# The lead of a top-k attention and mixture-of-experts kernel: the order of the first key and weight pieces

## The chip, the cores and the metric

The kernel runs on one core of a Trainium2 chip. The metric is the device time of one execution in microseconds, as a median over repeated runs. One further execution was taken by the hardware profiler, and all rows below are from that one.

## The reference

Three layers follow one another: attention that keeps only the 32 largest scores of each row, a dense layer that takes the larger of three products, and a layer of eight experts of which each token uses one.

```python
# q, k, v: (4, 8, 576, 64); out: (2304, 512)
scores = scale * np.matmul(q, k.transpose(0, 1, 3, 2))
kth = np.partition(scores, -top_k, axis=-1)[..., -top_k:-top_k + 1]      # top_k = 32
scores = np.where(scores >= kth, scores, -1e9)
attn = np.exp(scores - np.max(scores, axis=-1, keepdims=True))
attn = attn / (np.sum(attn, axis=-1, keepdims=True) + 1e-09)
x = np.matmul(attn, v)                          # heads side by side: (2304, 512)
h = np.maximum(np.maximum(x @ w1, x @ w2), x @ w3)                        # 512 -> 768
x = h @ w_out                                                             # 768 -> 512
logits = x @ w_gate                                                       # 8 experts
expert_idx = np.argmax(logits, axis=1)
# each token: gate_w * (max(x @ w1[e], 0) @ w2[e]) for its one expert e (512 -> 1024 -> 512)
```

The dense weights arrive as 64-bit floats, since they were scaled by a 64-bit number. All else is 32-bit.

## The kernel before

The attention is cut into 144 tiles. A full tile is 128 query rows of one head of one batch entry; the last 64 rows of two heads make up a pair tile. Batch entry 0 comes first, and its first eight tiles are query block 0 of heads 0 to 7, so tile n is head n there. The main loop runs over a clock t, and each pass issues one step of each of many stages, each stage on another tile: the scores of tile t+2 (`st_scores`, L883), the copy of the scores of tile t+1 from PSUM to SBUF by ScalarE (`st_evac`, L896), the eight largest of six chunks of tile t on VectorE (`st_chunks`, L904), the rounds that go on from these, the mask, the exponential, the product with the values, and units of the two dense layers and of the experts. The order is written by hand. Each engine takes its own instructions strictly in the order in which they are issued, and waits in place where an input is missing; the same holds for the queue on SyncE that issues nearly all DMAs.

`after(n, f)` (L671) puts a step off to n clocks later, `bulk` and `tail_bulk` collect VectorE's instructions of one clock, and `run_bulk` (L695) issues them: those in `bulk` first, those in `tail_bulk` behind.

Keys, queries and weights are used as pairs of 16-bit numbers, a high part and a low part. A key or query piece takes four steps: a load into a staging tile (`stage_load`, `stage_load2`), the high part by ScalarE (L757), the low part by VectorE (L734 in the lead, L741 with one more ScalarE copy at L740 later on), and one clock later a DMA transpose that SyncE issues (L772, L779 and L793). The query gets a swapped copy by two more DMAs (L797), which ScalarE issues in the lead. `prep_k(b, i)` (L760) has five pieces for each batch entry: pieces 0 and 1 hold the first 512 keys of heads 0 to 3, pieces 2 and 3 those of heads 4 to 7, piece 4 the last 64 keys of all heads. They are called k0 to k4 below, and the first query piece is called q0.

A dense weight piece (`prep_w`, L835) is 512 columns of 64-bit numbers, 512 KB. There are 24 of them, called w0 to w23 below, and six buffers for their raw bits. VectorE rebuilds a 32-bit number by three integer instructions into PSUM (L859, L862, L864, the "bits"), one clock later ScalarE writes the high part (L868), and the low part is made in one of two ways: in the lead by VectorE (L870), later by a ScalarE copy into the raw buffer (L874) and a subtraction on GpSimd (L875). From t = 0 to 5 two weight pieces are loaded in each pass, later one; each is worked on one pass after it was loaded.

The lead (L1552 to L1576) is what runs at negative clocks ahead of the main loop. It starts the loads of q0, k4, k0, k1, k2 and k3 at once, then does one piece in each clock, then w0 and w1, and at clock -1 it issues the scores and the copy of tile 0. The high and low parts of the lead's pieces lie in work buffers (`split_tile`, L747): three of the kind "e" and two of the kind "f", so the sixth piece has to take the buffer of the fourth.

## Time and profile of the kernel before

| | |
|---|---|
| median of 3 runs | 956.38 us (955.54 to 957.42) |
| the profiled execution | 951.46 us, of which its span from first to last instruction is 949.7 us |
| mean granted TensorE clock | 0.960 of full speed |
| VectorE / TensorE / ScalarE / GpSimd busy | 80% / 79% / 73% / 64% of the span |

The page divides the span into engines' busy times. An average over stages says little here, since the first three quarters and the last quarter are worked by different engines; the stretches and the orders of time below show which. Times of rows are microseconds from the span's start, the end of a row's bracket names what ended the engine's idle time before the instruction. PE is TensorE, DVE is VectorE, ACT is ScalarE, POOL is GpSimd, SP is SyncE; a q behind the name marks what the engine's queue issues, DMAs above all.

### The profile page before, as it was taken

The page shows a single profiled execution, that of the slowest core. Times are in us where ns is not written, and L with a number is a line of the kernel's source. Part 1 is how long each engine was busy: PE and PEld are TensorE (multiplying, and loading weights), DVE is VectorE, ACT ScalarE, POOL GpSimd, SP SyncE. Part 2 cuts the span into 40 slices and gives each one's busy share as a digit, 9 for nine tenths or more (in the row PEclk, how much of TensorE's full clock was granted, in tenths as well). Part 3 has the DMA queues.
Part 4 walks back from the last instruction along what each step waited for, and adds up shares of the span by engine and source line. Part 5 has one row for each costly group of instructions (what it writes and reads, how often), then busy time and mean ns, then how long its engine had stood idle before and what let it go on. Part 6 is the DMA issues. An engine that isn't in the chain of part 4 may idle for free. (4 is left out here: it accounts for less than half of the span.)

```text
span 949.7 us, 29065 instructions
## 1 busy us (share of the span) xinstructions
PE 751.6 (79%) x10606; PEld 578.1 (61%) x10606; DVE 762.5 (80%) x3110; ACT 694.3 (73%) x1463; POOL 608.6 (64%) x552
## 2 busy tenths in 40 slices
PE   0212368888777899878898998889999999999992
PEld 0100237666555677657677787567887767588881
DVE  4999999999998999998998899788972335567671
ACT  2668899997898988898897997887863231466661
POOL 1457798998988789787877898687985221111110
PEclk9999999999998999899989999889999999999996
DMA  9681977775996788699969888687799358699270
GB/s 229 204 260 29 223 158 153 138 143 105 184 165 151 143 161 175 111 206 176 173 128 179 170 139 154 131 188 127 170 168 156 91 150 278 177 299 279 63 216 16
DMA packets 372164, 155.93 MB, mean 164 GB/s; under 512 B 331931, under 2 KB 348319, under 8 KB 372000
## 3 DMA queue, kind: packets, MB, share of 16 engines
q1 hardware_dynamic: 368128, 143.10, 71.9%
q0 software_dynamic: 3136, 9.46, 2.8%
q8 instruction: 87, 1.43, 0.6%
q10 hardware_dynamic: 736, 1.32, 0.5%
q14 instruction: 77, 0.63, 0.3%
HBM read 76.06 MB, written 16.67 MB: 98 GB/s over the span
## 5 line engine op out<-in xcount | busy, mean ns | idle before, releaser
L355 PEld LDWEIGHTS <-W 128*128 128x128 f16 x4560 | 248.2, 100 | 28.0 <-issue 25.2
L965 POOL TENSOR_TENSOR f<-s,g 128x576 f32<-128x576 f32 x144 | 200.9, 1395 | 69.6 <-DVE vec L974 32.9
L355 PE MATMUL mm<-xT,W 128*128 128x128 f16 x3456 | 210.5, 222 | 18.2 <-DVE W1h L741 6.8
L1058 POOL TENSOR_TENSOR phl<-e,phl 128x576 f16<-128x576 f32 x144 | 186.3, 1293 | 8.1 <-ACT phl L1054 7.9
L913 DVE MAX8 c<-s 128x8 f32<-128x96 f32 x864 | 175.2, 243 | 8.3 <-ACT s L899 4.7
L892 PEld LDWEIGHTS <-qT 128*128 128x128 f16 (+1 forms) x640 | 56.3, 108 | 188.9 <-issue 156.6
L892 PE MATMUL S<-kt,qT 128*128 128x64 f16 (+3 forms) x320 | 62.4, 345 | 109.9 <-ACT s L899 94.4
L1077 PE MATMUL av<-vh,pt 128*128 128x65 f16 (+3 forms) x1600 | 112.4, 201 | 17.4 <-DVE xn L1126 12.9
L1043 ACT ACTIVATE e<-s,be 128x576 f32<-128x576 f32 x144 | 110.6, 768 | 7.7 <-POOL phl L1058 5.7
L974 DVE MAX8 vec<-f 128x8 f32<-128x576 f32 x144 | 108.8, 755 | 5.3 <-POOL f L965 1.4
L959 ACT ACTIVATE g<-s,bf 128x576 uint16<-128x576 f32 x144 | 111.1, 771 | 0.1
L1048 DVE SCALAR_TENSOR_TENSOR e<-s,hkth,e 128x576 f32<-128x576 f32 x72 | 104.1, 1446 | 8.3 <-ACT e L1043 8.1
L1077 PEld LDWEIGHTS <-pt 128*128 128x128 f16 (+3 forms) x2400 | 90.8, 104 | 30.5 <-issue 17.6
L1054 ACT ACTIVATE phl<-e 128x576 f16<-128x576 f32 x144 | 97.4, 676 | 11.3 <-DMA pt<-phl 11.3
L899 ACT ACTIVATE s<-S 128x576 f32<-128x576 f32 x144 | 92.3, 641 | 15.5 <-PE S L892 14.6
L1077 PE MATMUL av<-vl,pt 128*128 128x64 f16 (+3 forms) x800 | 101.6, 199 | 0.0
L1037 POOL TENSOR_TENSOR s<-s,g 128x576 f32<-128x576 f32 x72 | 95.9, 1331 | 0.3
L456 DVE SCALAR_TENSOR_TENSOR W<-st,W 128x1024 f16<-128x1024 f32 x56 | 65.8, 1220 | 36.7 <-ACT W L455 34.6
L892 PE MATMUL S<-kT,qT 128*128 128x512 f16 (+3 forms) x320 | 48.5, 293 | 18.7 <-ACT s L899 18.7
L455 ACT ACTIVATE W<-st 128x1024 f16<-128x1024 f32 x56 | 55.6, 1046 | 1.8 <-DMA st<-in_moe_w_dram 1.8
L1034 ACT ACTIVATE g<-s,hkth 128x576 uint16<-128x576 f32 x72 | 55.4, 769 | 0.0
L1161 POOL TENSOR_TENSOR hhl<-a,hhl 128x384 f16<-128x384 f32 x36 | 34.7, 964 | 28.9 <-ACT hhl L1160 28.9
(232 smaller groups left out, 1586.4 us busy)
## 6 DMA issues: line engine op xcount, KB each, us to landing
st<-in_moe_w_dram SPq DMA_DIRECT2D x72, 512.0 KB
st<-in_moe_w_dram SPq DMA_DIRECT2D x28, 256.0 KB
raw<-in_moe_w_dram SPq DMA_DIRECT2D x12, 512.0 KB
st<-in_v_dram SPq DMA_DIRECT2D x16, 256.0 KB
hs<-he SPq DMA_DIRECT2D x16, 256.0 KB
hTe<-hs SPq DMA_DIRECT2D x8, 512.0 KB
st<-in_q_dram SPq DMA_DIRECT2D x15, 256.0 KB
qT<-qT SPq DMA_DIRECT2D x30, 128.0 KB
```

The costliest lines, as they stand in the source:

```text
L355: nc.tensor.matmul(out=ps[:, o * n:(o + 1) * n], lhsT=w(b, kk, c), rhs=x(a, kk), start=(kk == 0 and i == 0), stop=(kk == KD - 1 and i == 2))
L892: nc.tensor.matmul(out=ps[o:o + m, j, 0:(REM if j else NQ * P)], lhsT=qt[:, vv, hh, 0:m], rhs=kr[:, hh] if j else km[:, hh // HG, :, hh % HG],
L913: nc.vector.max(out=c[:, i * 8:(i + 1) * 8], in_=s[:, i * CW:(i + 1) * CW])
L959: nc.scalar.activation(out=gg[n], in_=Ss[n], func=ACTF.Sign, bias=bf[g][:, i], accum_out=cnt[g][:, i])
L965: nc.gpsimd.tensor_tensor(out=ff[n], in0=Ss[n], in1=gg.pop(n).bitcast(F16), op=ALU.subtract)
L974: bulk.append(lambda: nc.vector.max(out=y8[g][:, i, 1:9], in_=y))
L1037: nc.gpsimd.tensor_tensor(out=Ss[n], in0=Ss[n], in1=zz.pop(n).bitcast(F16), op=ALU.subtract)
L1043: nc.scalar.activation(out=e, in_=Ss.pop(n) if early(n) else Ss[n], func=ACTF.Exp, scale=ESC, bias=be[g][:, i])
L1048: nc.vector.scalar_tensor_tensor(out=e, in0=Ss.pop(n), scalar=kth[g][:, i:i + 1], in1=e, op0=ALU.is_ge, op1=ALU.mult)
L1054: nc.scalar.activation(out=ph[:, 0, 0:S], in_=p, func=ACTF.Copy)
L1058: nc.gpsimd.tensor_tensor(out=ph[:, 1, 0:S], in0=p, in1=ph[:, 0, 0:S], op=ALU.subtract)
L1077: nc.tensor.matmul(out=av[o:o + m, i, 0:n], lhsT=t[0:kk, p * NCH + c, o:o + m], rhs=v_rows(x, b, c, hh)[:, 0:n], start=(c == 0 and p == 0 ...
```

## The change

The lead starts the loads of q0, k4, k0 and k1, then of w0, then of k2. It works through these six in the order q0, k4, k0, k1, w0, k2, one in each clock from -8 on. At clock -4 it starts the loads of w1 and of k3, and leaves their remaining steps to the main loop: both are worked on in the pass t = 0, and k3 is transposed in the pass t = 1. The branch by which VectorE made the low parts of the lead's weight pieces is gone, so w0 and w1 take the way of the others: a ScalarE copy and a subtraction on GpSimd.

```diff
--- before.py
+++ after.py
@@ -61,7 +61,7 @@
     NSWAP, XLAG, KLAG, TSTOP, EARLY_RATE, LATE_RATE = 4, 2, 2, 140, 1.4, 1.8
     RANK_LAG = 1
     ZN, NFB, NGB = (2,), 2, 4
-    NWL, WARM, ST = 2, 4, 3
+    WARM, ST = 4, 3
     ESC = 1.0 / (float(D) ** 0.5 * SC * SC * DOWN)
     LSC = 1.0 / (SC * SC)
     X2SC = 1.0 / (SC * SC)
@@ -855,7 +855,6 @@
                     lw, hw = raw[:, :, 0], raw[:, :, 1]
                     f = ps_m.tile([P, 512], F32, tag="mm", name="bits")
                     bits = f.bitcast(I32)
-                    head = clock[0] < 0
                     bulk.append(lambda: nc.vector.tensor_scalar(
                         out=bits, in0=hw, scalar1=3, scalar2=0x3FFFFFF8,
                         op0=ALU.logical_shift_left, op1=ALU.bitwise_and))
@@ -866,10 +865,6 @@
 
                     def rest():
                         nc.scalar.activation(out=dst[:, 0], in_=f, func=ACTF.Copy, scale=SC)
-                        if head:
-                            nc.vector.scalar_tensor_tensor(out=dst[:, 1], in0=f, scalar=SC, in1=dst[:, 0],
-                                                           op0=ALU.mult, op1=ALU.subtract)
-                            return
                         whole = raw.rearrange("p f w -> p (f w)")[:, 0:512].bitcast(F32)
                         nc.scalar.activation(out=whole, in_=f, func=ACTF.Copy, scale=SC)
                         nc.gpsimd.tensor_tensor(out=dst[:, 1], in0=whole, in1=dst[:, 0], op=ALU.subtract)
@@ -1533,6 +1528,10 @@
             preps.sort(key=lambda it: it[0])
             wq = [(prep_w, (i,)) for i in range(NPW + KF)]
 
+            def begin_w():
+                f, a = wq.pop(0)
+                return f(*a)
+
             def ok(n):
                 return 0 <= n < NTL
 
@@ -1549,13 +1548,20 @@
                 for ph in phl:
                     nc.gpsimd.memset(ph[:, :, S:SPAD], 0.0)
 
+                def begin(it):
+                    return it[2](*it[3])
+
                 lead = [it for it in preps if it[0] < 0]
                 lead.sort(key=lambda it: (it[2] is prep_k, (it[3][1] + 1) % (NQ + 1) if it[2] is prep_k else 0))
-                clock[0] = -len(lead) - 4
-                pend, pend_p, pend_w, lead_w, wq_n = [], [], [], [], [0]
                 for it in lead:
                     preps.remove(it)
-                    pend.append(it[2](*it[3]))
+                rows = lead[0], lead[1], lead[2], lead[3]
+                rest_k = lead[4:]
+                clock[0] = -8
+                pend_p, pend_w = [], []
+                pend = [begin(it) for it in rows]
+                pend.append(begin_w())
+                pend.append(begin(rest_k[0]))
                 while clock[0] < 0:
                     if clock[0] == -1:
                         st_scores(0)
@@ -1564,16 +1570,13 @@
                         f()
                     if pend:
                         pend.pop(0)()
-                    elif lead_w:
-                        lead_w.pop(0)()
-                    if len(pend) < NWL and wq_n[0] < NWL:
-                        wq_n[0] += 1
-                        f, a = wq.pop(0)
-                        lead_w.append(f(*a))
+                    if clock[0] == -4:
+                        pend_w.append(begin_w())
+                        pend_p.append(begin(rest_k[1]))
                     run_bulk()
                     run_late()
                     clock[0] += 1
-                assert not (pend or lead_w or any(c < 0 for c in due))
+                assert not (pend or any(c < 0 for c in due))
                 st_scores(1)
                 t = -1
                 second = None
```

## Rows read from the trace of the kernel before

**Rows 1.** The page's part 1: busy time, share of the span, instructions of each engine.

```profile
PE 751.6 (79%) x10606; PEld 578.1 (61%) x10606; DVE 762.5 (80%) x3110; ACT 694.3 (73%) x1463; POOL 608.6 (64%) x552
```

**Rows 2.** Busy time by stretch: start:end, length, each engine's busy us (instructions), clock, DMA.

```profile
23.60:100.00 76.40, 17.67 (x75) 7.67 (x75) 73.87 (x264) 55.02 (x122) 44.20 (x38) 1.00 0.59 172
...
700.00:800.00 100.00, 99.61 (x1250) 73.38 (x1247) 36.95 (x142) 33.46 (x66) 35.79 (x43) 1.00 0.65 154
```

**Rows 3.** VectorE's waits from 23.6 to 700: us in total, times, longest.

```profile
DVE bits L859 <- DMA raw<-in_moe_w_out_dram: 0.9, 1, 0.9
```

**Rows 4.** Order of time, ScalarE, 7 to 25: start, us, line, names, idle before.

```profile
7.15 0.63 ACT L757 ACTIVATE f<-s 128x512 f16<-128x512 f32 x1 [0.21 <-DMA s<-in_k_dram]
8.00 0.63 ACT L757 ACTIVATE f<-s 128x512 f16<-128x512 f32 x1 [0.22 <-DMA s<-in_k_dram]
9.64 1.18 ACTq L797 DMA_DIRECT2D qT<-qT  x2
15.26 0.63 ACT L757 ACTIVATE f<-s 128x512 f16<-128x512 f32 x1 [6.63 <-DMA kt<-f]
18.95 0.60 ACT L868 ACTIVATE W<-bits 128x512 f16<-128x512 f32 x1 [3.06 <-DVE bits L864]
22.37 0.60 ACT L868 ACTIVATE W<-bits 128x512 f16<-128x512 f32 x1 [2.82 <-DVE bits L864]
22.86 0.64 ACT L899 ACTIVATE s<-S 128x576 f32<-128x576 f32 x1
24.72 0.65 ACT L899 ACTIVATE s<-S 128x576 f32<-128x576 f32 x1 [1.21 <-PE S L892]
```

**Rows 5.** Order of time, SyncE's DMA issues, 5 to 13 (the same columns).

```profile
5.43 1.59 SPq L793 DMA_TRANSPOSE qT<-e  x1
...
9.77 1.44 SPq L779 DMA_TRANSPOSE kt<-f  x1
11.26 1.03 SPq L844 DMA_DIRECT2D raw<-in_moe_w_dram  x1
```

**Rows 6.** Order of time, VectorE, 23 to 43 (the same columns).

```profile
23.61 1.05 DVE L913 MAX8 c<-s 128x8 f32<-128x96 f32 x6
25.40 0.42 DVE L913 MAX8 c<-s 128x8 f32<-128x96 f32 x2 [0.74 <-ACT s L899]
...
26.77 0.68 DVE L859 TENSOR_SCALAR bits<-raw 128x512 int32<-128x512 int32 x1
...
28.86 0.69 DVE L859 TENSOR_SCALAR bits<-raw 128x512 int32<-128x512 int32 x1
...
30.91 0.41 DVE L913 MAX8 c<-s 128x8 f32<-128x96 f32 x2
...
39.87 0.69 DVE L859 TENSOR_SCALAR bits<-raw 128x512 int32<-128x512 int32 x1
...
41.92 0.68 DVE L741 TENSOR_TENSOR hl<-mm,hl 128x512 f16<-128x512 f32 x1
```

**Rows 7.** Busy time by stretch, 8 to 30 (last two columns: DMA share, GB/s).

```profile
8.00:15.00 7.00, 0.00 (x0) 0.00 (x0) 1.19 (x2) 0.63 (x1) 0.00 (x0) 1.00 1.05 195
15.00:20.00 5.00, 1.12 (x4) 0.56 (x5) 3.20 (x5) 1.23 (x2) 0.00 (x0) 1.00 1.14 269
20.00:25.00 5.00, 1.12 (x4) 0.46 (x4) 3.92 (x11) 1.42 (x3) 0.00 (x0) 1.00 0.93 329
25.00:30.00 5.00, 2.24 (x8) 0.91 (x8) 4.57 (x18) 2.04 (x4) 0.00 (x0) 1.00 1.10 346
```

**Rows 8.** Order of time, GpSimd and VectorE, 26 to 39.

```profile
26.22 0.19 DVE L929 MATCH_REPLACE8 c<-T,c 128x48 f32<-128x48 f32 x1
...
36.64 2.27 POOL L875 TENSOR_TENSOR W<-raw,W 128x512 f16<-128x512 f32 x2 [1.77 <-DMA raw<-in_moe_w_dram]
...
37.24 0.19 DVE L929 MATCH_REPLACE8 c<-T,c 128x48 f32<-128x48 f32 x1
```

**Rows 9.** Order of time, TensorE: the scores of tile 4.

```profile
32.81 1.12 PE L892 MATMUL S<-kt,qT 128*128 128x512 f16 x4 [4.42 <-ACT s L899]
```

## The prediction

> **What bounds the kernel now.** First the page's table of engines: VectorE is busy for 80% of the span and TensorE for 79% [rows 1], which as an average names no bound. The table by stretch does: from 23.6 to 100 VectorE works 73.87 of 76.4 us while TensorE works 17.67, and from 700 to 800 TensorE works 99.61 of 100 [rows 2]. So VectorE sets the pace from the main loop's start on, and TensorE near the end. The list of VectorE's waits adds that in 676 us it waited for a load only once, for 0.9 us [rows 3]: what VectorE has to do, and when it may begin, decides, not the DMAs.
>
> When it may begin is read from ScalarE's order of time [rows 4]. The high part of k3 starts only at 15.26, after 6.63 us of idling for a key transpose: its buffer is that of k1, and k1's transpose had to land first. That transpose also completes the keys of tile 0, whose scores could therefore be copied out some 1.2 us later. Instead the copy starts at 22.86, because ScalarE's order puts the high parts of k3, w0 (18.95) and w1 (22.37) ahead of it, and both weights wait about 3 us for VectorE's bits. VectorE's first chunks follow at 23.61 and the pass t = 1 begins at 25.40 [rows 6]. The time between 15.3 and 22.9 is what the change can reach.
>
> **The change part by part.** I follow VectorE up to the first chunks of tile 1, since from there on its list of instructions is the old one.
>
> *k1's transpose.* Ahead of the transposes the queue now carries w0 (512 KB) in place of k3 (256 KB). The high parts of k1 and k2, each released by its load, start 0.85 us apart, 7.15 and 8.00 [rows 4]: 0.85 us for each 256 KB. The issue times don't move, since SyncE waits for low parts anyway: q0's transpose is issued at 5.43, k1's at 9.77, one weight load takes 1.03 us to issue [rows 5]. If the transposes start moving when the loads are through, everything behind shifts by one such step, and k1 lands at 15.26 + 0.85 = 16.11. The ends: no shift, if the queue has slack (from 8 to 15 it moved 195 GB/s at a DMA share of 1.05, so I doubt it [rows 7]), and 1.70, if all of w0 counts. A gain is excluded here, as nothing ahead of k1's transpose but k3's load goes away. I take 0.85.
>
> *The copy and the chunks of tile 0.* From a released score to its copy takes 1.21 us, the wait ahead of the copy at 24.72; from a copy to its chunks 25.40 - 24.72 = 0.68 [rows 4, 6]. So the copy starts at 16.11 + 1.21 = 17.32 and the chunks at 18.00. What ScalarE has ahead of this copy is done by then: w0 lands two steps after k1, at 7.15 + 1.70 = 8.85; three bits take 30.91 - 28.86 = 2.05 [rows 6]; the swap, at 9.64 before, shifts to 10.49 and takes 1.18 to issue; then come two copies for w0 (0.60 each) and the high part of k2 (0.63) [rows 4], until 13.5. Cover 3.8 us; past it, every us counts in full.
>
> *The pass t = 0.* VectorE now does six chunks (1.05), the bits of w1 (2.05) and the low part of k3 (0.68) [rows 6]: 18.00 + 3.78 = 21.78. Before, t = 1 began at 25.40. The gain is **3.62 us**.
>
> *GpSimd.* Two low parts leave VectorE and become two ScalarE copies (about 0.60 each) and two subtractions of 2.27 / 2 = 1.13 us [rows 4, 8]. The first lies ahead of tile 0's copy (within the 13.5 above), the second in t = 1, where ScalarE has only the copy of tile 2 besides. GpSimd has nothing else there. I cost this at nothing; without cover on ScalarE it is 1.2 us.
> The row that matters for VectorE: a match-replace beside a running subtraction took 0.19 us at 37.24, and 0.19 at 26.22 with GpSimd idle [rows 8]. The Trainium skill speaks against this part (SBUF — State Buffer, section "SBUF: two separate sides"): GpSimd and VectorE share a port pair, and a VectorE instruction with two SBUF inputs blocks against a GpSimd one that reads SBUF. By that page up to one subtraction would be added to t = 1; the trace shows no such lengthening.
>
> *New waits.* (a) ScalarE in t = 0: the high part of k3 waits for its load, and the copy of tile 1 stands behind it. After k1's transpose come w1 and k3, 0.79 MB; at 269 GB/s, the rate of the stretch 15 to 20 [rows 7], 2.9 us, so 19.0; then 0.63, 0.60 and the copy's 0.65: 20.9, with 21.78 wanted. Free by 0.9 us; at 195 GB/s it would cost 0.2. (b) SyncE in t = 1: the transpose of k3 waits for its low part until 21.78, and behind it stand the loads of w4 and w5, of the next query and value pieces, and of w6 and w7. (c) TensorE: tile 4 is the first to need k2 and k3. Its scores ran at 32.81 [rows 9]; shifted by 3.6 they are due at 29.2. k1's transpose took 15.26 - 9.77 = 5.5 us from issue to landing [rows 4, 5], so k3's lands by 27.3: nothing; if later, TensorE waits, and the chunks of tile 4 are still two passes off.
>
> For (b), count what must pass the queue from 16.11 until the bits of w7, at 39.87 before and so due at 21.78 + (39.87 - 25.40) = 36.25 [rows 6]: seven pieces of 512 KB (w1 to w7) and five of 256 KB (k3, two transposes, a query and a value piece), 4.98 MB in 20.14 us, or 247 GB/s. From 15 to 30 the queue moved 269, 329 and 346 [rows 7], on average 315, which does it in 15.8 us: 4.3 us to spare.
>
> *Sum.* The pass t = 1 begins 3.6 us earlier, and with it everything: from there on the instructions and their order are the old ones, no engine looks at a clock on the wall, and the loads keep up. Against the profiled execution: 951.46 - 3.6 = 947.9. That execution is 4.9 us below the median of the runs; the shift is a sum of durations, so I carry it over: 956.38 - 3.6 = **952.8 us**. By the ends of k1's landing 951.9 (no shift) to 953.6 (1.70).
>
> **The rivals.**
>
> *Starved a little.* The loads of w2 to w7 fall behind as in (b): at 225 GB/s the 4.98 MB take 22.1 us, 2.0 more than there is, and 954.8 is left. For it: SyncE stands still behind k3's transpose for some us. Against: 315 GB/s measured with two transposes among the traffic.
>
> *Starved for good, slower than before.* The same place: if the queue only keeps the 195 GB/s that it had beside the transposes and the swap from 8 to 15 [rows 7], 25.5 us are needed, 5.4 too many; 958.2. Below 210 GB/s the gain is gone, below 194 the kernel is slower by more than 0.2%.
>
> *The copy stays late: the change doesn't do what it says.* ScalarE's copy of tile 0 now stands behind w0's high part. If w0's 512 KB came only after the transposes, 2.7 us behind 16.11 at 195 GB/s, the bits would end at 20.9, ScalarE would reach the copy at 22.7, and w1 and k3 (2.73 us) would still lie in t = 0: t = 1 at 23.4 + 3.78 = 27.2, 1.8 late, 958.2. It decides from an arrival of w0 after 13.5. Against: k1 and k2 arrived in the order of their issue, 0.85 apart.
>
> *Taken up later.* The last quarter is TensorE's [rows 2]; if its work there doesn't start earlier, 956.4 stays. Against: its inputs come from the stages that shift, in the same order.
>
> *GpSimd holds VectorE up.* In t = 1 the subtraction for w1 delays VectorE by its own 1.13 us: 953.9. Against: the 0.19 beside 0.19 above. It is what the page named there would have.
>
> **How the numbers follow.** Forecast 62%, starved a little 13%, taken up later 14%, the copy late 5%, starved for good 4%, GpSimd in the way 2%. A measurement of this kernel can tell about 0.2%, 1.9 us, from no change; the runs before spread by 0.9 us to either side. Faster: the forecast but for 1%, half of the little starvation (6%) and GpSimd in the way, rounded to 69%. Same: taken up later, the other half, and a part of the late cases, 24%. Slower: the rest, 7%. The range runs from the forecast's best end less 0.9, 951.0, to the case taken up later plus 0.4, 956.8; the two late cases are left out, and a remainder at either edge.
>
> **What would show it.** In the order of time after: the first copy at L899 at 17.3 (16.5 to 18.2) and not behind a wait for bits; the first chunks at 18.0; t = 1's chunks at 21.8; no L870 any more; the scores of tile 4 near 29.2 without a wait for a transpose; no VectorE wait for raw weight loads ahead of 40. It would be wrong if ScalarE idles ahead of the high part of k3 until after 20, if VectorE waits at L859 in the first four passes, or if the distance to the old trace, 3.6 at t = 1, shrinks later on.

## The result, and the profile after

The kernel after takes 948.59 us (946.08 to 951.09, 11 runs) where the kernel before took 955.54 (950.67 to 961.45, 11 runs) beside it on the same chip: a ratio of 0.9913, with a 95% interval of 0.9888 to 0.9938. That is 7 us less by the medians and 8.3 by the ratio, faster as forecast, but about twice the forecast gain of 3.6, and the time lies below the forecast range. The profiled execution took 946.08 us (span 944.4, mean granted clock 0.965) against 951.46.

The page's engine table hardly moves; it is the line that answers to [rows 1].

```profile
PE 747.3 (79%) x10606; PEld 576.8 (61%) x10606; DVE 764.4 (81%) x3108; ACT 695.9 (74%) x1466; POOL 611.3 (65%) x554
```

Busy time by stretch, from the first chunks on and near the end (start:end, length, then PE, PEld, DVE, ACT and POOL busy, clock, DMA share, GB/s), answers to [rows 2]: VectorE still works nearly without a break at the start (80.79 of 83.3 us), TensorE in the last quarter.

```profile
16.68:100.00 83.32, 19.75 (x94) 9.12 (x94) 80.79 (x284) 60.87 (x133) 48.84 (x43) 1.00 0.70 190
700.00:800.00 100.00, 99.63 (x1174) 70.92 (x1172) 39.48 (x171) 28.30 (x57) 28.72 (x37) 1.00 0.68 172
```

ScalarE in order of time (start, us, line, names, idle before), for [rows 4]. The swap is issued 1.2 us later than before, the copy of tile 0 (L894) starts at 15.99 in place of 22.86 and waits only for its scores, and the high part of k3 (the line of 17.48) waits 0.84 us for its load.

```profile
10.85 1.24 ACTq L797 DMA_DIRECT2D qT<-qT  x2
12.13 0.60 ACT L867 ACTIVATE W<-bits 128x512 f16<-128x512 f32 x1 [4.16 <-DVE bits L863]
...
13.10 0.63 ACT L757 ACTIVATE f<-s 128x512 f16<-128x512 f32 x1
15.99 0.65 ACT L894 ACTIVATE s<-S 128x576 f32<-128x576 f32 x1 [2.25 <-PE S L887]
17.48 0.63 ACT L757 ACTIVATE hl<-s 128x512 f16<-128x512 f32 x1 [0.84 <-DMA s<-in_k_dram]
```

TensorE in order of time, for [rows 9]: the scores of tile 0, released by k1's transpose at 14.83, and those of tile 4, which wait for ScalarE's freeing of their buffer as before and not for k3's transpose.

```profile
14.83 1.12 PE L887 MATMUL S<-kt,qT 128*128 128x512 f16 x4 [14.83 <-DMA kt<-f]
...
27.69 1.12 PE L887 MATMUL S<-kt,qT 128*128 128x512 f16 x4 [5.07 <-ACT s L894]
```

VectorE in order of time, for [rows 6]: the chunks of tile 0 at 16.67, the bits of w1 and the low part of k3, the pass t = 1 at 20.29, and the pass t = 2 at 25.80.

```profile
16.67 1.06 DVE L908 MAX8 c<-s 128x8 f32<-128x96 f32 x6 [1.67 <-ACT s L894]
17.65 0.67 DVE L858 TENSOR_SCALAR bits<-raw 128x512 int32<-128x512 int32 x1
...
20.29 0.41 DVE L908 MAX8 c<-s 128x8 f32<-128x96 f32 x2
...
25.80 0.41 DVE L908 MAX8 c<-s 128x8 f32<-128x96 f32 x2
```

So the start came out 1.5 us better than forecast. To see what became of it, take the first chunk instruction of each tile (L913 before, L908 after) and subtract the two traces: -5.11 us at tile 1, -4.39 at tile 16, -4.35 at tile 40, then **-8.44 at tile 48**. (Why 0.7 us of the first distance go between tiles 1 and 16 was not followed up.) Between tiles 40 and 48 the two kernels issue the same instructions in the same order, and yet 4.1 us go there that nobody forecast. This subtraction is quoted below for each kernel.

Here is that place in the kernel before: VectorE, in order of time.

```profile
209.27 0.13 DVE L1246 TENSOR_REDUCE si<-vec 128x1 int32<-128x8 f32 x1
209.86 0.77 DVE L974 MAX8 vec<-f 128x8 f32<-128x576 f32 x1 [0.46 <-DVE si L1246]
...
210.71 1.37 DVE L1048 SCALAR_TENSOR_TENSOR e<-s,hkth,e 128x576 f32<-128x576 f32 x1
...
214.97 7.09 DVE L1048 SCALAR_TENSOR_TENSOR e<-s,hkth,e 128x576 f32<-128x576 f32 x1
221.98 0.20 DVE L932 MAX8 T<-c 128x8 f32<-128x48 f32 x1
```

And GpSimd beside it, in the same kernel; L1257 is the indirect DMA by which a tile's rows are scattered to their experts' places ("the scatter" below, 18 of them in the stage in question).

```profile
210.56 0.90 POOL L1161 TENSOR_TENSOR hhl<-a,hhl 128x384 f16<-128x384 f32 x1
...
214.63 1.18 POOL L1257 DMA_INDIRECT xs<-xr,si  x1 [0.17 <-issue]
215.84 1.28 POOL L1037 TENSOR_TENSOR s<-s,g 128x576 f32<-128x576 f32 x1
...
220.18 1.26 POOL L1037 TENSOR_TENSOR s<-s,g 128x576 f32<-128x576 f32 x1
```

The same instructions of VectorE and of GpSimd in the kernel after.

```profile
205.16 0.77 DVE L969 MAX8 vec<-f 128x8 f32<-128x576 f32 x1
...
206.01 0.84 DVE L1043 SCALAR_TENSOR_TENSOR e<-s,hkth,e 128x576 f32<-128x576 f32 x1
...
209.74 0.97 DVE L1043 SCALAR_TENSOR_TENSOR e<-s,hkth,e 128x576 f32<-128x576 f32 x1
```

```profile
206.19 1.43 POOL L1156 TENSOR_TENSOR hhl<-a,hhl 128x384 f16<-128x384 f32 x1
...
210.26 1.49 POOL L1252 DMA_INDIRECT xs<-xr,si  x1 [0.17 <-issue]
211.79 1.29 POOL L1032 TENSOR_TENSOR s<-s,g 128x576 f32<-128x576 f32 x1
```

Read them in pairs. The instruction that decides is VectorE's mask (L1048 before, L1043 after), which reads two SBUF tiles. Before, VectorE stands still for 0.46 us ahead of the MAX8 at 209.86, where the kernel after has 0.10 us: a pause of 0.35 us, for no release that the profile shows. By that the mask at 210.71 comes just behind a GpSimd subtraction (210.56) and takes 1.37, while the subtraction takes 0.90. After, there is no pause, the mask comes first (206.01 against 206.19), takes 0.84, and it is the subtraction that is stretched, to 1.43. Whoever is first has its way, the other waits. VectorE is now 0.86 us later against GpSimd before than after, and at the next mask that turns the order round once more: before, it starts 0.34 us behind the scatter and takes 7.09 us; after, it starts 0.52 us ahead of it and takes 0.97. In the kernel before GpSimd works on from 214.63 to 221.44 without a gap, and the mask ends 0.62 us after that: it waited until GpSimd had nothing more to do. Not all of this lasts. The two traces are 11.35 us apart at tile 44 and 8.44 at tile 48, because VectorE of the kernel after then idles 1.12 us for an exponential and its next mask takes 2.25 us in place of 0.81.

The Trainium skill ("SBUF — State Buffer", section "SBUF: two separate sides") has a rule for this: a VectorE instruction with two SBUF inputs and a GpSimd instruction that reads SBUF exclude one another, and the one that starts first keeps the shared ports for its whole instruction. The pair 1.37/0.90 against 0.84/1.43 agrees. The 7.09 goes further than the page: this wait lasted through the scatter and five subtractions, not through one instruction.

### The profile page after: what moved, and what is told of

Its sections match the earlier page's. It is cut to its first block, busy times and chain, and to the rows that moved or that the text cites. A ratio compares the mean times of both kernels' runs of the same rounds, so it can differ in the third digit from the quotient of the medians.

```text
span 944.4 us, 29070 instructions
## 1 busy us (share of the span) xinstructions
PE 747.3 (79%) x10606; PEld 576.8 (61%) x10606; DVE 764.4 (81%) x3108; ACT 695.9 (74%) x1466; POOL 611.3 (65%) x554
## 3 DMA queue, kind: packets, MB, share of 16 engines
q8 instruction: 87, 1.43, 0.7%
HBM read 76.06 MB, written 16.67 MB: 98 GB/s over the span
## 5 line engine op out<-in xcount | busy, mean ns | idle before, releaser
L355 PE MATMUL mm<-xT,W 128*128 128x128 f16 x3456 | 213.0, 223 | 21.8 <-DVE W1h L741 6.0
L908 DVE MAX8 c<-s 128x8 f32<-128x96 f32 x864 | 175.5, 244 | 6.7 <-ACT s L894 2.8
L1043 DVE SCALAR_TENSOR_TENSOR e<-s,hkth,e 128x576 f32<-128x576 f32 x72 | 105.5, 1465 | 8.6 <-ACT e L1038 4.4
L894 ACT ACTIVATE s<-S 128x576 f32<-128x576 f32 x144 | 92.2, 641 | 8.0 <-PE S L887 7.0
L355 PEld LDWEIGHTS <-W1e 128*128 128x128 f16 x864 | 50.3, 99 | 5.1 <-issue 3.1
```

Source lines behind the costliest of these rows:

```text
L355: nc.tensor.matmul(out=ps[:, o * n:(o + 1) * n], lhsT=w(b, kk, c), rhs=x(a, kk), start=(kk == 0 and i == 0), stop=(kk == KD - 1 and i == 2))
L908: nc.vector.max(out=c[:, i * 8:(i + 1) * 8], in_=s[:, i * CW:(i + 1) * CW])
L1043: nc.vector.scalar_tensor_tensor(out=e, in0=Ss.pop(n), scalar=kth[g][:, i:i + 1], in1=e, op0=ALU.is_ge, op1=ALU.mult)
```

## The experiments

Two theories were open. **A**: the gain is that of the start alone, carried through one to one, and what comes on top is chance in later stages. **B**: a second term of about 4 us near tile 41 comes on top; in its sharper form **C**: it is the long mask, and it hangs on the pause, and so on how many instructions VectorE's list has (3427 before, 3425 after, since two low parts left it), not on when the kernel starts. The table gives the median of each kernel, its ratio to the kernel before on the same chip (954.66 us for the first four rows, 956.16 for the next four, then 953.79 and, for the last three, 953.90), and the shift of VectorE's chunks against the trace of before.

| kernel | median us (runs) | ratio, 95% interval | tile 1 | tile 40 | tile 48 |
|---|---|---|---|---|---|
| again | 946.79 (6) | 0.9911, 0.9882 to 0.9939 | -4.53 | -4.06 | -8.14 |
| after_late | 949.71 (12) | 0.9958, 0.9936 to 0.9980 | +1.21 | +2.13 | -1.96 |
| before_late | 959.21 (12) | 1.0051, 1.0027 to 1.0075 | +5.45 | +5.41 | +5.40 |
| w1_early | 948.55 (10) | 0.9931, 0.9908 to 0.9954 | -2.91 | -2.03 | -6.12 |
| pad2 | 949.38 (6) | 0.9923, 0.9901 to 0.9945 | -4.25 | -3.97 | -3.97 |
| gp_alone | 952.01 (7) | 0.9947, 0.9923 to 0.9970 | -0.15 | -0.12 | -4.21 |
| order_alone | 944.92 (6) | 0.9891, 0.9855 to 0.9927 | -4.73 | -4.76 | -8.86 |
| w0_behind | 953.56 (1) | none | -0.02 | +1.28 | -2.80 |
| late_put | 943.12 (6) | 0.9903, 0.9874 to 0.9931 | -4.93 | -4.37 | -8.26 |
| late_put_order | 941.70 (6) | 0.9898, 0.9874 to 0.9923 | -5.21 | -4.69 | -8.57 |
| swap_behind | 949.59 (1) | none | -0.90 | -0.65 | -0.57 |
| before_pad2 | 951.02 (12) | 0.9968, 0.9942 to 0.9994 | -0.57 | -0.11 | -4.23 |
| late_put_before | 947.37 (6) | 0.9922, 0.9892 to 0.9951 | +0.25 | +0.22 | -3.87 |
| after_swap_behind | 948.42 (1) | none | -2.61 | -1.19 | -5.27 |
| swap_behind_late_put | 944.90 (1) | none | -0.84 | -0.06 | -4.16 |

(A ratio is made of the runs of both kernels that belong together, so it need not be the quotient of the medians.)

### Start and rest apart

The first kernel is the changed one once more, to see how far two executions differ. 

> The changed kernel once more, in five rounds beside the kernel before. Theory A (only the start counts): in the profiled pair VectorE's chunks ran 4.4 us ahead from tile 16 to tile 40, and the 7 us between the medians are 4.4 us and scatter of the runs; it gives about 4.4 us less than before (3.5 to 5.5), ratio 0.9954. Theory B (the change also speeds up the rest): 7 us less again, ratio 0.993.

The gain is there again, with the same two steps: -4.06 at tile 40, -8.14 at tile 48. Tile 1 differs by 0.6 us from one execution to the next, since k1's transpose landed at 15.41 here and at 14.83 there.

In two kernels only the start is moved: tile 0 is copied out nine times in place of once (eight idle repeats of the same copy), in the one kernel and in the other.

```diff
...
                     if clock[0] == -1:
                         st_scores(0)
+                        for _ in range(8):
+                            st_evac(0, again=True)
                         st_evac(0)
```

> The changed kernel with its start put off: ScalarE copies tile 0 out nine times instead of once, about 0.54 us each, so that VectorE's first chunks come near 21.0 instead of 16.7 and the pass t = 1 near 24.6, within 1 us of the kernel before. Theory A: the time of the kernel before within 1 us. Theory B: still 2 to 3 us less than before.

> The kernel before with tile 0 copied out nine times instead of once: its pass t = 1 begins 4.3 us later, near 29.7. Theory A: 4.3 us more than before, ratio 1.0045. A rival, that the stages behind have slack and swallow a late start: under 2 us more.

The kernel before, 5.4 us late at tile 1, is 5.40 late at tile 48 and 4.9 us (0.51%) longer: what is lost or won at the start does go through one to one, as the forecast had it, and its 7.09 us mask stays where it was, 5.4 us later. The changed kernel with a start that is no longer early (+1.21, +2.13 at tile 40) still drops by 4.1 us between tiles 40 and 48 and stays faster than before, by 0.42%. Theory A falls: the 4.1 us do not come from the early start.

### What the 4.1 us hang on

Two more short VectorE copies, beside idle time at 3.4 us, bring the changed kernel's list back to the old length:

```diff
-            nc.vector.tensor_copy(out=vhalf.bitcast(I32), in_=dhalf)
+            for _ in range(2+1):
+                nc.vector.tensor_copy(out=vhalf.bitcast(I32), in_=dhalf)
```

> The changed kernel with two short VectorE copies repeated among the constants at 3.4 us, where VectorE idles: its instruction list has as many instructions again as that of the kernel before, and the lead is unchanged. Theory C (where VectorE's program is refilled): the two kernels before (before, before_late) pause VectorE for 0.36 us at its 831st instruction, near tile 41, lose the port to GpSimd there and fall 4.1 us behind; the four kernels with the change, two VectorE instructions shorter, don't. So pad2 should pause there again, be 4.4 us ahead of before up to tile 40 and only 0.3 ahead at tile 48: about 4 us slower than the changed kernel, ratio to before 0.9955. Theory D (two more instructions on GpSimd, or anything else of the lead, does it): as the changed kernel, 8 ahead at tile 48, ratio 0.991.

VectorE of pad2 near tile 41, in order of time: the pause is back, and the mask of 7.09 us is back, with the early start untouched. Its shift is -3.97 both at tile 40 and at tile 48. (The 0.3 that was expected at tile 48 forgets that the kernel before has the long mask as well; with a start 4.4 us early theory C gives about 4.4 there.) The time does not follow: the ratio is 0.9923 where theory C had 0.9955, which lies outside the interval, so that pad2 bears theory C out up to tile 48 and not at the end.

```profile
205.89 0.77 DVE L970 MAX8 vec<-f 128x8 f32<-128x576 f32 x1 [0.46 <-DVE si L1242]
...
210.99 7.09 DVE L1044 SCALAR_TENSOR_TENSOR e<-s,hkth,e 128x576 f32<-128x576 f32 x1
```

The opposite is the kernel before with nothing but the low parts of w0 and w1 given to GpSimd, the lead's order left as it was:

```diff
...
-                        if head:
-                            nc.vector.scalar_tensor_tensor(out=dst[:, 1], in0=f, scalar=SC, in1=dst[:, 0],
-                                                           op0=ALU.mult, op1=ALU.subtract)
-                            return
```

> The kernel before with one part of the change: GpSimd makes the low parts of w0 and w1, the order stays. For the lead: VectorE's two low parts go, ScalarE gets two copies ahead of tile 0's copy, so the pass t = 1 begins within 0.6 us of before. The prediction's sum gives no change (ratio 1.000, within 0.6 us). Theory C: VectorE's list is two instructions shorter, so the stall near tile 41 goes, 4 us less, ratio 0.996, though the lead is as long as before.

The start doesn't move (-0.12 at tile 40), the pause and the long mask are gone, tile 48 is 4.21 us early, and the median is 4.15 us below that of the kernel before. This half of the change alone is worth 4 us, by way of two instructions that are missing some 800 instructions earlier.

The other half, the order alone, with the low part of w0 left to VectorE (so that its list is one shorter than before):

```diff
...
+                        if head:
+                            nc.vector.scalar_tensor_tensor(out=dst[:, 1], in0=f, scalar=SC, in1=dst[:, 0],
+                                                           op0=ALU.mult, op1=ALU.subtract)
+                            return
```

> The changed kernel with the other part alone: the low part of w0 is VectorE's again (w1, worked on in the main loop, stays with GpSimd). VectorE idles between 11.2 and 13.8, so tile 0's chunks and the pass t = 1 should stay within 0.5 us of the changed kernel (or 0.6 earlier: one ScalarE copy fewer ahead of k2). By the start alone: as the changed kernel. By theory C its VectorE list is one instruction shorter than before, and whether the pause shows at tile 41 is open: 8 ahead of before at tile 48 if not, 4 if so.

It has the start's gain (-4.76 at tile 40, 0.4 more than the kernel after) and no pause there either, so it has all of the 8.9 us at tile 48. GpSimd's low parts thus give the start nothing that shows.

Two copies more in the kernel before make its list two longer than ever:

> The kernel before with two more short VectorE copies (the constant's copy done three times, at about 3.4 us, beside idle time): VectorE's list is two longer, so each pause of its program comes two instructions earlier in the work. Theory C in its form of a place: the pause of 0.40 us is at the 831st record as ever, but that is now an instruction two earlier in tile 40; whether the mask still starts behind the indirect DMA hangs on whether the pause still stands between the two, and it does (two MAX8 earlier, same pass): the mask of 7.1 us stays, 954 to 958. Theory that any change of the list's length frees the mask: no mask over 4 us near 211 to 216, 951 to 953. Theory that VectorE's list has nothing to do with it: 954 to 958 with the pause where it was, at the 833rd record.

Of its three expectations the second came true: no pause at that MAX8, masks of 0.83 and 0.98 us, tile 48 at -4.23. It isn't that a longer list is worse; only the old length has the pause just there. Over all seventeen traces it stands ahead of that MAX8 in the six whose VectorE list has 3427 instructions (before, before_late, pad2, swap_behind, late_put_before, swap_behind_late_put; an early or a late start makes no difference) and in none of the eleven with 3425, 3426 or 3429. What makes the pause isn't settled. Packets of the queue that the page calls "instruction" lie beside it (210.1 and 210.5 in the kernel before), which could speak for a refill of VectorE's program. But they start behind the pause, and the kernel after has such packets beside the same MAX8 (205.7 and 206.7) without a pause, so they don't decide it.

### The scatter's place

If the long mask comes from standing just behind the scatter, the scatter can be put elsewhere: at the end of its pass, behind the other work.

```diff
-                        nc.gpsimd.indirect_dma_start(
+                        late.append(lambda: nc.gpsimd.indirect_dma_start(
                             out=xs, out_offset=bass.IndirectOffsetOnAxis(ap=si[:, :1], axis=0),
                             in_=j.xr, in_offset=None, bounds_check=NXS - 1, oob_is_err=False,
-                        )
+                        ))
```

> The kernel after, with the rank scatter (GpSimd's indirect DMA of xr into xs, 18 of them) put at the end of its pass, behind the other work of that pass, in place of its middle. Theory C (a mask of VectorE that starts 0.3 to 0.9 us behind such a DMA waits for the whole run of GpSimd work behind it): the masks over 4 us that start so (four in the kernel after: 6.93, 4.57, 5.07, 5.07, 4.67 among them) fall away or become rare, each worth about 4 us net, so 8 to 16 us: 932 to 941. Rival (the long masks come from GpSimd's run of subtractions alone, wherever the scatter stands): as many masks over 4 us as before the edit, at the same or shifted places, and the time stays within 2 us of the kernel after, 945 to 950. A third way: the scatter meets the next pass's mask or MAX8 instead, and the later landing of xs holds up nothing (it is read only after the last tile): 945 to 950 too, with the long masks at other tiles.

> The kernel with the new order alone (the first weight piece's low part still by VectorE) with the rank scatter at the end of its pass. Theory C: 930 to 939, as in the kernel with both; if the pause of VectorE's program falls badly again, 4 us more. Rival (scatter's place doesn't matter): 943 to 947.

> The kernel before with the rank scatter (the indirect DMA of xr into xs) at the end of its pass. Theory C (the change's gain is 4.4 us of an earlier start, carried through, and about 4 us of one long mask near tile 41 that the scatter's place and VectorE's list bring about): the mask of 7.1 us near 215 is gone, VectorE's chunks of tile 48 are 4 us ahead of the kernel before and 4.2 to 4.7 behind late_put's, and the time is 945 to 949, some 4.4 above late_put's 943.1. Rival (the change's gain beyond the start comes from something else than this mask): the mask is gone or not, and the distance to late_put stays 7 or more, 950 to 954. Rival (the start's gain is taken up later): within 2 us of late_put, 941 to 945.

The masks (72 in each kernel) as one group, from the page's fifth part: the kernel after, then late_put (busy us, then mean ns).

```profile
L1043 DVE SCALAR_TENSOR_TENSOR e<-s,hkth,e 128x576 f32<-128x576 f32 x72 | 105.5, 1465 | 8.6 <-ACT e L1038 4.4
```

```profile
L1043 DVE SCALAR_TENSOR_TENSOR e<-s,hkth,e 128x576 f32<-128x576 f32 x72 | 90.8, 1261 | 8.5 <-ACT e L1038 8.2
```

Six masks of the kernel after took over 4 us: five of them started 0.33 to 0.86 us behind the start of a scatter (6.93, 4.57, 5.07, 5.07 and 4.67 us), one (6.22) had none near. In late_put one mask over 4 us is left (4.85), and it has no scatter near. The kernel before with the scatter moved, late_put_before, still has the pause, but loses its 7.09 too (the mask at 215.18 takes 1.34 us; -3.87 at tile 48, start unmoved). So what brings most of the long masks about is shown: the place just behind the scatter. This place is neither needed nor enough. The mask of 6.22 has no scatter near, and another of the kernel after that starts 0.76 us behind a scatter takes 0.80. What the eleven long masks of the kernels before and after share is that each waits through several GpSimd instructions without a gap between them and ends 0.62 to 0.63 us behind the last of these; why other masks get their turn behind the first is open.

It also agrees with the sum. With the scatter out of the way in both, the changed kernel is ahead by 8.26 - 3.87 = 4.39 at tile 48: the start's gain and nothing else. Up to there the two parts of the change's gain are therefore 4.3 us of start, and some 4 us of one mask. The times don't settle it by themselves: the medians differ by 947.37 - 943.12 = 4.25 us, but the ratios, 0.9922 and 0.9903, by 1.8 us, with intervals that overlap.

late_put and late_put_order are about 1% faster than the kernel before. That they are faster than the kernel after isn't shown: their medians are 3.7 to 6.9 us lower than those of after and again, which did not run beside them, but the ratios (0.9903 and 0.9898 against 0.9913 and 0.9911) differ by 1.5 us at most, inside the intervals. Both medians lie above what theory C forecast and below the rival's. The 14.7 us by which the two groups above differ are no fixed price either: again, which is the same kernel as after, has 94.5 us in this group, and the kernel before 104.1. So where the masks lose time changes from one execution to the next, and of the long ones only that near tile 41 follows VectorE's list in every trace that has the scatter in place. GpSimd and VectorE of late_put show one place where time is lost instead:

```profile
499.45 1.01 POOL L1252 DMA_INDIRECT xs<-xr,si  x1 [11.85 <-DMA mte<-xs]
```

```profile
501.81 0.77 DVE L969 MAX8 vec<-f 128x8 f32<-128x576 f32 x1 [5.74 <-POOL f L960]
```

One of the moved scatters now stands behind a load that reads the same tensor, keeps GpSimd idle for 11.85 us, and VectorE, which waits for a GpSimd result queued behind it, for 5.74. A version that moves the others and not this one wasn't tried.

### The landing of k1's transpose

The forecast had it at 16.11; it came at 14.83. The suspect is the query's swap (L797, 256 KB on ScalarE's queue), whose packets share the DMA engines with the transposes. In the kernel before they ran right among them: queues in the stretch 11 to 12 (packets, MB, time as a share of 16 engines).

```profile
q10 hardware_dynamic: 70, 0.11, 62.6%
q1 hardware_dynamic: 282, 0.07, 35.2%
```

q10 is the swap, q1 carries loads and transposes. In the kernel after, the same stretch has no q10 packet at all (139 of its 160 come from 13 to 14), and q1 moves 997 packets:

```profile
q1 hardware_dynamic: 997, 0.25, 118.5%
```

The Trainium skill ("DMA: Bandwidth & Descriptors", section "Queues, rings and completion order") says that a DMA engine takes turns between the queue rows that have work, a packet at a time. The stretch agrees in that both queues go on together, and q1 moves 282 packets in it where it moves 779 and 713 in the stretches beside it.

To measure it the swap alone is put off by one step of the lead's clock, in the kernel before and in the kernel after:

```diff
-                    after(5 if early_q else 2, swap)
+                    after(6 if early_q else 2, swap)
```

> The kernel before, with the query's swap (and with it the issue of what follows it on ScalarE's queue) put off by one step of the lead's clock, to behind k1's high part. It tells how much of k1's transpose's early landing in the new order comes from the swap no longer running among its packets. Theory of the swap: tile 0's scores start at 14.3 to 14.9 (before: 15.32). Theory of the loads alone (0.85 us for each 256 KB ahead, none of it moved here): 15.3 or later, and tile 0 up to 0.8 us later if the swap itself is what the scores wait for. Time 954 to 957 by both.

> The kernel after with the query's swap put off by one step of the lead's clock, as in swap_behind. In swap_behind k1's transpose landed at 12.90; here 256 KB more of loads stand ahead of it. Theory of the loads (0.85 us for each 256 KB): it lands at 13.7 to 13.8. Theory that the loads ahead cost nothing, the transposes being late for another reason: 12.9. Theory that the swap is not what the landing hangs on: 14.8 to 15.7, as in the kernels with the new order. Tile 0's copy waits for the swap in any case, so tile 0 comes no earlier and perhaps 1 to 3 us later than in the kernel after: 946 to 950.

> swap_behind with the rank scatter at the end of its pass too. For the start it is a second look at swap_behind: k1's transpose lands at 12.7 to 13.3 if the swap is what the landing hangs on, at 14.5 or later if swap_behind's 12.90 was scatter. For the time: 944 to 949, some 4 us below swap_behind, with no mask over 6 us near tile 41.

ScalarE of swap_behind in order of time: the high part of k3, released by k1's transpose, starts at 12.90 in place of 15.26.

```profile
12.90 0.63 ACT L757 ACTIVATE f<-s 128x512 f16<-128x512 f32 x1 [4.21 <-DMA kt<-f]
12.93 1.18 ACTq L797 DMA_DIRECT2D qT<-qT  x2
```

TensorE of the same kernel: tile 0's first score matmul at 12.96, the others only when the swap has landed.

```profile
12.96 0.59 PE L892 MATMUL S<-kt,qT 128*128 128x512 f16 x1 [12.96 <-DMA kt<-f]
18.66 0.69 PE L892 MATMUL S<-kt,qT 128*128 128x512 f16 x3 [5.11 <-DMA qT<-qT]
```

swap_behind_late_put landed at 12.96 as well, earlier than even the theory of the swap had it (14.3 to 14.9): the swap costs the transpose 1.6 to 2.6 us in the old order, where it lands at 14.58 to 15.56 (five traces). With the swap put off in the new order too, k1 lands at 14.71 (after_swap_behind), 1.75 later than in the old order: that is the price of the 256 KB more ahead of it, near the upper of the forecast's two ends (1.70), and a little too high still, as 32 packets of the swap fall between 13 and 14 there. Most of it is a later issue: SyncE issues k1's transpose at 11.27 there, and at 9.69 in swap_behind. The theory of 0.85 is wrong, and so is the one of nothing. In the new order the swap costs little: this one trace, at 14.71, is hardly earlier than the earliest of the kernels with the swap in its place (14.73 to 15.70), and 0.5 us earlier than their mean.

The two nearly cancel, and one can see it in the other traces too, in the two steps from the swap's issue to the landing. In five traces of the old order the swap was issued at 9.50 to 9.96 (mean 9.67) and k1 landed 5.32 later on average; in eight of the new one it was issued at 10.64 to 11.74 (mean 11.16) and k1 landed 4.07 later. So 1.49 us go with the later issue, and 1.25 come back behind it. In the mean k1 lands at 15.23 in the new order and at 14.99 in the old one: early against the forecast, but not against the kernel before.

### Two other orders

One puts the bits of w1 ahead of tile 0's chunks, between its copy and them:

```diff
+                    if clock[0] == -2:
+                        pend_w.pop(0)()
                     run_bulk()
                     run_late()
```

> The changed kernel with VectorE's three bit instructions of w1 ahead of the chunks of tile 0 (its high and low parts stay behind the copy of tile 0): VectorE idles for 1.7 us there. If w1 has landed by 15.3, the chunks of tile 0 begin near 17.4 instead of 16.7 and the pass t = 1 near 19.1 instead of 20.3, so 1.2 us less than the changed kernel by theory A. If w1 lands only after 17, nothing is gained or up to 1 us is lost.

VectorE then waits 2.19 us for w1, which lands at 17.57, and the first chunks move from 16.67 to 19.63 and the pass t = 1 from 20.29 to 22.49, so 2.2 us are lost where up to 1 was expected. The other puts the load of w0 behind k1's transpose and that of k2 ahead:

```diff
-                pend.append(begin_w())
                 pend.append(begin(rest_k[0]))
...
+                    if clock[0] == -4:
+                        pend.insert(0, begin_w())
                     if pend:
                         pend.pop(0)()
```

> The changed kernel with the load of w0 begun only behind k1's transpose, and k2's ahead. It asks why k1's transpose landed at 14.8 and not at 16.1. The prediction's rule (0.85 us for each 256 KB of loads ahead of the transposes): 512 KB less, so it lands 1.7 us earlier, near 13.1. The rival (what holds k1's transpose is the query's swap, whose 256 KB ran ahead of it in the kernel before and behind it in the changed one): q0 lands early again, near 9.6, the swap goes ahead of k1's transpose again, and this lands at 14.0 or later. Tile 0's copy waits for w0 then, so the first chunks come later than 16.7.

Here k1 lands at 14.29, only about 0.9 us ahead of the other traces of the new order, since the swap is issued at 9.13 and so runs among the transposes again. But w0's bits wait until 16.79, VectorE idles for 8.13 us, tile 0 is copied at 20.47, and tile 1 has no gain left (-0.02). It is the rival "the copy stays late" made real: had w0 come late, the gain would have gone.

### The end

What a kernel has at tile 48 isn't quite what it has at the end. Of the nine kernels with several runs that leave the scatter in place (the kernel after among them), the difference of the medians lies between 3 us below and 1.5 above the shift at tile 48. By the ratios the kernel after and again are 8.3 and 8.5 us faster, which is the whole shift at tile 48; by the medians 7.0 and 7.9. Pad2 is a case that the theory doesn't explain: by tile 48 alone it should stand at 952, and it has 949.4. Other masks come to stand behind or ahead of the scatter later on (the kernel before has five over 4 us, the kernel after six, again three), and one execution differs from the next there. One term of the end has a row: TensorE's wait for the experts' rows between 800 and 820 (us in total, times, longest), in the kernel before, after and late_put.

```profile
PE ph L355 <- DMA W1h<-xs: 2.1, 1, 2.1
```

```profile
PE ph L355 <- DMA W1h<-xs: 2.8, 1, 2.8
```

```profile
PE ph L355 <- DMA W1h<-xs: 5.1, 1, 5.1
```

The earlier TensorE gets there in these three, the longer it waits, so this part of the gain is given back. After the wait of 2.8 us the granted clock of the kernel after averaged 0.66 in the stretch 810 to 815, so it stood at the lower level (1.2 GHz) for part of it; in the kernel before it was 1.00 from 800 to 830. Between the same matmuls, those at 802 and 834 of the kernel before, the profiled execution after lost 2.1 of its 9.0 us, and that of late_put 4.7 of its 13.6.

## Why the prediction was right or wrong

**What bounds the kernel: right.** The start of VectorE's list is what the change could reach, and an earlier or later start arrives at the end (before_late: 5.4 in, 4.9 out).

**k1's transpose: the term was mis-sized.** It was put at 15.26 + 0.85 = 16.11 and came at 14.83. On average over eight traces it came at 15.23, which is 0.24 later than the 14.99 of the old order, inside the forecast's ends (0 to 1.70), but by luck, as two larger terms nearly cancel. The price of the loads was too low (1.5 to 1.75), and "the issue times don't move" was wrong: k1's transpose is issued at 10.33 in place of 9.77, in the mean of these traces at 10.66 in place of 9.79. And "a gain is excluded here" counted only what stands ahead on SyncE's queue, and not the swap on ScalarE's, although the forecast itself let the swap shift by 0.85. [Rows 7] had the hint, 195 GB/s at a share of 1.05 in the stretch where both queues ran.

**Copy, chunks and the pass t = 0: right.** From landing to copy 1.16 (1.21 forecast), from copy to chunks 0.68 (0.68), ScalarE free at 13.73 (13.5), t = 0 took 20.29 - 16.67 = 3.62 (3.78). The pass t = 1 began at 20.29 in place of 21.78, and 1.28 of these 1.49 us are k1's landing.

**The new waits: right.** The high part of k3 at 17.48, free as forecast; the transpose of k3 holds up no score of tile 4; VectorE waited for raw bits once, for 1.4 us, where [rows 3] had 0.9, and not in the first passes. The queue kept up.

**GpSimd and VectorE: the price in t = 1 was right, the reason against the rule was not.** The pass t = 1 takes 25.80 - 20.29 = 5.51 us, as it did before (30.91 - 25.40), with the subtraction for w1 in it. But the row that was held against the page on the shared ports, a match-replace of 128x48 in 0.19 us, says nothing about a mask of 128x576. On the masks the rule holds (1.37 against 0.84), and it was looked for in the first pass only, because the change puts its subtraction there.

**"From there on the instructions and their order are the old ones", so all shifts one to one: this step failed.** It is the larger half of the miss. The instructions are the old ones, but two fewer stand ahead of them on VectorE, a pause of 0.35 us no longer falls where it did, and a mask that started 0.34 us behind the scatter starts 0.52 us ahead of it: 7.09 against 0.97 us, 4.1 us net at tile 48. As far as the change is concerned this half of the gain is luck: nothing in it was meant for that mask, and two idle copies take it away again at tile 48 (pad2). The sum of what was shown, 4.35 (start, at tile 40) and 4.1 (mask), is 8.4; measured were 7.0 and 7.9 by the medians of the kernel after and of again, 8.3 and 8.5 by the ratios. Apart from the mask the distance did shrink too, from 5.11 at tile 1 to 4.35 at tile 40, which the prediction named as a sign of being wrong; its cause is open.

**The rivals.** None of the five came true. Starved, late copy and taken up later all made the gain smaller; the possibility of a second gain from the same port that the last rival feared wasn't among them, and the range ended at 951.0 for that reason. A forecast could have seen the place: the row of 7.09 us stood in the trace of before, one of five masks over 4 us. It could not have told from that trace which way a change of the list's length would turn it.

## What to carry to other kernels

Look for the longest instructions of a group whose shortest ones are much shorter: where the shortest masks take 0.80 us and five in 72 take 4.9 to 7.1, look at what GpSimd does beside them, and where a scatter is followed by a run of subtractions, try the scatter at another place. Here that removed all but one of the long masks, though what it is worth in the end is shown against the kernel before only. When a lead is reordered, list the transfers of all queues that run at the same time as the one that counts, since a transfer moved out of its way can be worth more than the bytes put ahead of it. And a change of a few instructions on one engine can turn a race with another engine for or against it, by some 4 us here; such a spread belongs into the range, on both sides.

## What the runs showed of the hardware that was not expected

- A VectorE instruction with two SBUF inputs that started 0.34 us behind the start of an indirect DMA of GpSimd waited through that DMA and the five back-to-back subtractions behind it, took 7.09 us in place of 0.84 to 0.97, and ended 0.62 us after GpSimd fell idle. A mask can wait as long without such a DMA (6.22 us through five subtractions in the kernel after), while another (1.37 us), behind a subtraction that a further one followed without a gap, lost only 0.53 us.
- VectorE paused 0.35 us with nothing to wait for that the profile shows, at the same instruction in all six traces whose list has 3427 instructions, and not there in the eleven with other numbers.
- A 256 KB SBUF-to-SBUF copy on a second queue made a DMA transpose land 1.6 to 2.6 us later in the old order (five traces against two), and hardly later in the new one (0.5 us in the mean).
